# Last two chunks of a gated scan: transposing the input instead of the norm, with a new order of the tail

## The chip, the cores and the metric

The kernel runs on one core of a Trainium2 chip. The metric is the device time of one execution in microseconds; the runs shown have 290.55 us as their median. A core has five engines that each work through their own instructions in order and wait for one another by semaphores: PE (matrix multiplies and transposes, which write to the PSUM banks), DVE (elementwise work and scans), ACT (functions by table, copies), POOL (elementwise work in SBUF) and SP, which here issues the DMA transfers.

## What is computed

Two stages on an input of 4 sequences, 6336 steps and 256 channels. The first is a gated linear recurrence along the steps, the second a gated unit with a causal convolution of 5 taps:

```
log_a = 8 * sigmoid(r_gate) * log(clip(sigmoid(a_param)))
a     = exp(log_a)
norm  = sqrt(max(1 - a*a, 1e-6))
h[t]  = a[t] * h[t-1] + norm[t] * sigmoid(i_gate[t]) * x[t]      # attn_out = all h
gate  = sigmoid(causal_conv(attn_out, conv_w))                   # 5 taps per channel
out   = (gate * (attn_out @ w_val)) @ w_out
```

## The kernel before

The 25344 steps (all sequences in a row) are cut into 51 windows, w0 to w50, of 512 steps (w0, w1 and w50 have 256). The windows form 28 chunks: chunks 0, 1 and 2 have one window each, chunks 3 to 25 have two (w3 and w4, up to w47 and w48), chunk 26 is w49 and chunk 27 is w50. Steps arrive with time on the partitions and channels along the row; the scan needs channels on the partitions, so data is transposed on PE. The 256 channels are two halves h of 128.

Every piece of work is a word in the string ORDER. The kernel goes through the string from left to right and emits each word's instructions; each engine then runs its own words in that order, and waits are inserted where a word reads or overwrites what another engine has not finished. There is no planner at run time: the string is the schedule. A word is a name, its indices and, after @, the PSUM banks (0 to 7) that it fills. For window w, chunk c, half h:

- SP: lr, li, lx load a window of r_gate, i_gate and x (line 290); st.w stores a window of the output (line 519). Each load goes to a ring of 4 windows, each store leaves from a ring of 4.
- ACT: ta.c and tb.c take tanh of half the r and i gates (lines 308 and 311); ex.c.h takes exp out of PSUM into the ring of a (line 376); rt.b takes the square root of 1 - a*a for a batch of chunks (line 403; rt.10 covers chunks 23, 24 and 25, rt.11 chunks 26 and 27); tg.w takes tanh of the convolution (line 475); ca.w copies output out of PSUM (line 508); sa.c.h squares a (line 392). The square root is in another function table than tanh and exp, so each rt is enclosed by two table loads (line 535).
- POOL: pp.w adds one to the i gate (line 318), up.w multiplies it by x into the ring u (line 330), sq.c.h squares a (line 384).
- PE: tr.c.h transposes the r gate (line 355); nt.c transposes the norm back to time on partitions (line 418); xt.c transposes the gated input (line 434); cv.w is the convolution (line 468, 20 matmuls), vl.w the product with w_val (line 483, 4), ou.w the product with w_out (line 498, 8); wm are five matmuls whose result nobody reads (line 362).
- DVE: xg.c multiplies the transposed norm into u (line 425); sc.c.h scans one half of a chunk (line 456, into the ring of y); gv.w combines gate and value (line 488); cd.w copies output out of PSUM (line 506).

Two bfloat16 neighbours are moved as one 32-bit element in the transposes nt and xt, so a window of 512 steps takes 4 of each (two blocks by two halves), one of 256 takes 2.

For each chunk the way from the square root to the scan is: rt (ACT), nt (PE), xg (DVE, PSUM times u into u), xt (PE, into one bank for each half), sc (DVE, which reads a from SBUF and the gated input from PSUM). Then for each window cv and vl on PE, tg on ACT, gv on DVE, ou on PE, a copy, and the store. The y ring holds 3096 columns; chunk 26 starts again at its beginning, where its first scan also copies the last four columns of chunk 25 (line 451).

At the tail, chunks 26 and 27 go through rt.11, nt.26 and nt.27, xg.26 and xg.27, xt.26 and xt.27, sc.26 and sc.27; the last words are w50's: cv.50, tg.50, vl.50, gv.50, ou.50, ca.50, st.50.

Of the kernel before, what the change touches and what calls it, by code (L numbers as in the profile page):

```python
# [42 lines left out]
sc.0.0 up.3 nt.1@3 lx.5 nt.2@0 uv.1 s_wl.0 xg.1 xg.2 xt.1@2,3 lx.7 sc.0.1 lr.12 nt.3@0,1 sc.1.0 lr.11 xt.2@6,7
sc.1.1 ex.5.0 xg.3 tr.5.1@2,3 li.8 sc.2.0 xt.3@0,1 ex.5.1 sq.5.0 cv.0@4,5 sc.2.1 tg.0 sc.3.1 cv.1@6,7 cv.2@2,3 tg.1
tb.4 s_wcast xp.6@6,7 sc.3.0 tg.2 li.10 li.9 pp.5 ta.8 vl.1@4,5 lx.10 vl.2@2,3 uv.6 sq.6.1 vl.0@0,1 ta.7 gv.2 lr.17
cv.3@6,7 lx.8 sq.6.0 gv.0 ou.2.0@2,3 gv.1 tb.5 ou.0.0@0 cd.2.0 ou.1.0@1 up.5 tr.7.0@4,5 tg.3 cd.0.0 st.2 vl.3@2,3
lr.16 cd.1.0 ex.7.0 sq.5.1 st.1 tr.7.1@6,7 gv.3 lr.15 st.0 nt.4@0,1 li.12 ex.7.1 pp.7 cv.4@4,5 xg.4 sq.7.0
# [11 lines left out]
tg.13 sc.9.1 lr.29 pp.20 ou.12.0@0,1 ta.13 up.18 vl.13@6,7 cd.12.0 tr.12.1@3 tg.14 up.17 sc.9.0 st.12 tr.13.1@0,1
ex.12.1 lx.19 lx.20 nt.10@4,5 ex.13.1 li.24 sq.12.1 gv.13 tr.13.0@2,3 tb.12 xg.10 ou.13.0@6,7 sq.13.1 xt.10@4,5  # L60
cd.13.0 ex.13.0 cv.15@0,1 pp.22 sc.10.0 st.13 lx.21 cv.16@6,7 pp.19 lx.22 tg.15 lr.28 lr.30 sq.13.0 vl.15@2,3 tg.16
sc.10.1 li.25 vl.14@0,1 lr.27 pp.21 vl.16@6,7 gv.15 rt.6 sq.14.1 gv.14 ou.15.0@2,3 up.19 gv.16 cv.17@4,5 ou.14.0@0,1
cd.15.0 up.20 ou.16.0@6,7 cd.14.0 st.15 li.26 nt.11@2,3 cd.16.0 sq.14.0 lx.24 vl.17@0,1 tg.17 xg.11 st.14 lx.23
tb.13 st.16 gv.17 xt.11@2,3 up.21 cv.18@4,5 sc.11.1 sc.11.0 li.27 nt.12@0,1 li.28 ta.15 up.22 vl.18@6,7 tg.18 lr.32
pp.23 lr.31 ta.16 ou.17.0@4,5 pp.24 gv.18 up.24 tb.14 xg.12 tr.15.1@2,3 cv.20@6,7 cd.17.0 ex.15.1 xt.12@0,1 up.23
st.17 lr.33 tr.15.0@4,5 sc.12.0 lx.26 tg.20 lr.34 vl.20@2,3 sq.16.1 ex.15.0 cv.19@6,7 sc.12.1 sq.15.1 tg.19
ou.18.0@4,5 tb.15 cd.18.0 cv.21@0,1 pp.26 gv.20 st.18 sq.16.0 vl.19@4,5 tg.21 lx.25 lx.27 nt.13@6,7 ta.17 gv.19
lx.28 li.30 sq.15.0 vl.21@0,1 xg.13 li.29 ou.20.0@4,5 gv.21 xt.13@6,7 pp.27 rt.7 cv.22@2,3 cd.20.0 up.26 ou.21.0@0,1
# [498 lines left out]
```

## Time and profile before

| what | value |
|---|---|
| median of 3 runs | 290.55 us (290.2 to 290.71) |
| the profiled execution | 290.72 us |
| its span, first to last instruction | 288.6 us |
| granted PE clock, mean | 0.996 |
| busy: PE, DVE, ACT, POOL | 250.6, 247.0, 273.7, 241.5 us |
| HBM traffic | 362 GB/s over the span |

The profile is of one execution. Times in it are microseconds from the start of the span; the execution's own time is 2.1 us longer than the span. A row of a timeline gives start, duration, engine, line, operation, output and inputs, and how many instructions are merged; in brackets stands the idle time of the engine before it and what ended that. Instructions of one engine overlap a little, so the time that one holds its engine is read from its start to the next start. A merged row of matmuls is one word or several of the same kind: x8 at line 498 is one ou, x20 at line 468 one cv.

### The profile page before, as it was taken

Reading aid. Unit: us, or ns where it says so; the run is one execution under the profiler, and the core shown is the slowest. Engines: PE = TensorE matmul, PEld = TensorE weight load, DVE = VectorE, ACT = ScalarE, POOL = GpSimd, SP = SyncE. Lnnn points to the kernel's source line nnn. Section 1 sums busy time; section 2 is a strip of 40 time slices with the busy share of each in tenths; the row PEclk is TensorE's granted clock in tenths of the full one; section 3 lists DMA queues with packets and bytes.
Section 4 is the critical chain, followed back from the end, with each engine's and each line's share of the span. In section 5 each row is a group of like instructions: output and inputs, shape, how many; then the busy total and the mean of one; then the engine's idle time right before and its main releaser. Section 6 shows DMA issues by size and latency. Waiting matters only on the chain.

```text
span 288.6 us, 6363 instructions
## 1 busy us (share of the span) xinstructions
PE 250.6 (87%) x2552; PEld 169.4 (59%) x2552; DVE 247.0 (86%) x214; ACT 273.7 (95%) x197; POOL 241.5 (84%) x161
## 2 busy tenths in 40 slices
PE   2397799879898899889898999889799897999993
PEld 1253557547656677466567585467457664676552
DVE  5002899869999999999998999989999999999891
ACT  4999999999999999999999999999999999999754
POOL 1669469999999999999999999999998999496100
PEclk9999999999999999999999999999999999999998
DMA  7999999999999999999999999999999999885554
GB/s 240 396 392 409 407 374 385 357 385 371 403 407 410 410 395 366 375 346 417 418 408 341 376 413 414 418 395 396 351 352 412 420 386 408 263 292 208 199 221 182
DMA packets 29996, 104.76 MB, mean 363 GB/s; under 512 B 3335, under 2 KB 3854, under 8 KB 29966
## 3 DMA queue, kind: packets, MB, share of 16 engines
q1 hardware_dynamic: 29952, 104.35, 93.9%
q8 instruction: 20, 0.33, 0.5%
q14 instruction: 10, 0.08, 0.1%
q10 hardware_dynamic: 14, 0.01, 0.0%
HBM read 78.39 MB, written 25.95 MB: 362 GB/s over the span
## 4 chain that ended last, share of the span: by engine, by line
POOL 31%; PE 20%; DMA 15%; DVE 12%; ACT 12%; issue 7%; SPq 2%; DVEq 0%; ACTq 0%; POOLq 0%
POOL uring L330 14%; POOL ering L384 11%; DMA xring<-in_x_dram 8%; POOL tbring L318 6%; PE banks L468 6%; DMA iring<-in_i_gate_dram 6%; DVE yring L456 5%; DVE tgring L488 4%; PE banks L483 4%; PE banks L498 3%; PE banks L418 3%; ACT aring L376 3%; ACT tbring L311 3%; ACT ering L403 2%; SPq L290 2%
## 5 line engine op out<-in xcount | busy, mean ns | idle before, releaser
L330 POOL TENSOR_TENSOR uring<-tbring,xring 128x1024 bf16<-128x1024 bf16 (+1 forms) x48 | 100.9, 2116 | 11.1 <-DMA xring<-in_x_dram 10.6
L456 DVE TENSOR_TENSOR_SCAN yring<-aring,yring,banks 128x1024 bf16<-128x1024 f32 (+5 forms) x54 | 105.8, 1987 | 0.2
L384 POOL TENSOR_TENSOR ering<-aring 128x1024 f32<-128x1024 f32 (+2 forms) x54 | 91.7, 1715 | 14.7 <-ACT aring L376 14.6
L468 PE MATMUL banks<-yring,diag 64*64 64x512 bf16 (+7 forms) x1080 | 62.9, 361 | 4.6 <-DVE yring L456 3.6
L488 DVE SCALAR_TENSOR_TENSOR tgring<-tgring,banks 128x1024 bf16<-128x1024 bf16 (+1 forms) x51 | 59.3, 1178 | 5.1 <-PE banks L483 2.4
L498 PE MATMUL banks<-wo,tgring 128*128 128x256 bf16 x396 | 51.1, 274 | 7.5 <-DVE tgring L488 4.9
L376 ACT ACTIVATE aring<-banks,khf 128x2048 f32<-128x2048 bf16 (+3 forms) x38 | 53.9, 1467 | 0.4 <-PE banks L355 0.4
L475 ACT ACTIVATE tgring<-banks 128x1024 bf16<-128x1024 f32 (+1 forms) x51 | 50.5, 1007 | 3.0 <-PE banks L468 2.9
L318 POOL TENSOR_SCALAR tbring<-tbring 128x1024 bf16<-128x1024 bf16 (+1 forms) x48 | 49.0, 1030 | 4.4 <-ACT tbring L311 4.3
L498 PEld LDWEIGHTS <-tgring 128*128 128x128 bf16 x396 | 41.4, 114 | 18.6 <-DVE tgring L488 10.5
L483 PE MATMUL banks<-yring,wv 128*128 128x512 bf16 (+4 forms) x216 | 49.6, 361 | 1.6 <-ACT aring L376 0.8
L308 ACT ACTIVATE taring<-rring 128x2048 bf16<-128x2048 f32 (+2 forms) x28 | 47.6, 1718 | 2.4 <-DMA rring<-in_r_gate_dram 2.4
L311 ACT ACTIVATE tbring<-iring 128x2048 bf16<-128x2048 f32 (+2 forms) x28 | 47.9, 1719 | 0.0
L468 PEld LDWEIGHTS <-diag 64*64 64x64 bf16 x1080 | 29.1, 106 | 28.1 <-issue 11.6
L403 ACT ACTIVATE ering<-ering 128x4096 bf16<-128x4096 f32 (+5 forms) x15 | 44.7, 3016 | 0.1
L506 DVE COPY oring<-banks 128x1024 f32<-128x1024 f32 (+1 forms) x36 | 42.0, 1182 | 1.6 <-PE banks L498 1.1
L355 PE MATMUL banks<-ident_b,taring 128*128 128x128 bf16 x396 | 30.2, 230 | 9.4 <-ACT taring L308 7.2
L425 DVE TENSOR_TENSOR uring<-banks,uring 128x2048 bf16<-128x2048 bf16 (+2 forms) x28 | 30.4, 1093 | 6.7 <-PE banks L418 5.7
L355 PEld LDWEIGHTS <-taring 128*128 128x128 bf16 x396 | 26.1, 103 | 15.1 <-ACT taring L308 9.2
L483 PEld LDWEIGHTS <-wv 128*128 128x128 bf16 x216 | 19.9, 98 | 21.3 <-issue 7.1
L418 PE MATMUL banks<-ident,ering 128*128 128x128 f32 x198 | 29.7, 292 | 1.9 <-DVE yring L456 0.9
L418 PEld LDWEIGHTS banks<-ident,ering 128*128 128x128 f32 x198 | 25.9, 207 | 9.1 <-ACT ering L403 3.5
(45 smaller groups left out, 139.7 us busy)
## 6 DMA issues: line engine op xcount, KB each, us to landing
rring<-in_r_gate_dram SPq DMA_DIRECT2D x48, 512.0 KB, 7.9
iring<-in_i_gate_dram SPq DMA_DIRECT2D x48, 512.0 KB, 8.2
xring<-in_x_dram SPq DMA_DIRECT2D x48, 512.0 KB, 7.9
out_dram<-oring SPq DMA_DIRECT2D x48, 512.0 KB, 5.8
rring<-in_r_gate_dram SPq DMA_DIRECT2D x3, 256.0 KB, 4.4
iring<-in_i_gate_dram SPq DMA_DIRECT2D x3, 256.0 KB, 5.8
xring<-in_x_dram SPq DMA_DIRECT2D x3, 256.0 KB, 8.2
out_dram<-oring SPq DMA_DIRECT2D x3, 256.0 KB, 7.4
```

What stands on the lines that cost most here:

```text
L311: nc.scalar.activation(**tangent(c, tbring, NTI, iring, NII))
L318: nc.gpsimd.tensor_scalar(out=t, in0=t, scalar1=1.0, scalar2=1.0, op0=ALU.mult, op1=ALU.add)
L330: nc.gpsimd.tensor_tensor(out=u, in0=t1, in1=xt, op=ALU.mult)
L355: nc.tensor.transpose(out=bank[:, o:o + P], in_=taring[:, place(w, NTR), j, h * P:(h + 1) * P], identity=ident_b[:])
L376: nc.scalar.activation(out=dst, in_=src, func=ACT.Exp, scale=khf[:, h:h + 1], bias=khf[:, h:h + 1])
L384: nc.gpsimd.tensor_tensor(out=e, in0=a, in1=a, op=ALU.mult)
L418: nc.tensor.transpose(out=bank[:, k:k + P], in_=ering[:, e + q:e + wins[w] // 2:nq], identity=ident[:])
L456: nc.vector.tensor_tensor_scan(out=yring[:, h, col:col + o1 - o0], data0=aring[:, h, a_at[c] + o0:a_at[c] + o1], data1=xT[:, o0:o1], initi ...
L468: nc.tensor.matmul(out=gp[oh * 64:oh * 64 + 64, h, a:b], lhsT=diag[half * 64:half * 64 + 64, h, k, :], rhs=yring[half * 64:half * 64 + 64, ...
L483: nc.tensor.matmul(out=val[:, m, a:b], lhsT=wv[:, hk, m * P:(m + 1) * P], rhs=yring[:, hk, col:col + b - a], start=(hk == 0), stop=(hk == ...
L488: nc.vector.scalar_tensor_tensor(out=tgring[:, w % NTG, :, 0:wins[w]], in0=tgring[:, w % NTG, :, 0:wins[w]], scalar=1.0, in1=live.pop(("va ...
L498: nc.tensor.matmul(out=ops[:, j * D:(j + 1) * D], lhsT=gv[:, hk, j:wins[w]:J], rhs=wo[:, hk, :], start=(hk == 0), stop=(hk == H - 1))
```

## The change

For the last two chunks (LAST) the gated input u is transposed first, without the norm: xt.26 and xt.27 put both halves into one PSUM bank. xg.26 and xg.27 then multiply that bank by the norm as it stands (channels on partitions) and write the product into the y ring, at the columns where the chunk's y will stand. The scan reads it from there and overwrites it in place. nt.26 and nt.27 are gone. The other chunks work as before.

The order of the tail is new. Up to w35 each engine has the same words in the same order as before (banks 2, 3 and 4, 5 are exchanged in the middle part, and the words of different engines stand differently in the string). From there on:

- PE: vl.37 directly after nt.22, one new wm.19, and other places for ou, vl and cv up to nt.23; tr.27.0, tr.26.1, tr.27.1 and tr.26.0 later; xt.26 and xt.27 around cv.47, ahead of rt.11's result. From cv.49 on the order is as before.
- POOL: sq.24.0 after sq.25.0; at the end sq.27.0, pp.49, sq.26.1, up.49, pp.50, up.50, sq.26.0 (before: sq.26.1, sq.27.0, sq.26.0, pp.50, pp.49, up.49, up.50).
- ACT: rt.11 after tg.46 and before tg.47 (before: after tb.27 and before ca.42); ta.27, ta.26, the exps of chunks 26 and 27 and tb.27, tb.26 in other places.
- DVE: gv.42, gv.43 and gv.44 spread between the scans of chunks 23 and 24; at the end sc.25.0, sc.25.1, gv.45, gv.46, xg.27, xg.26, sc.26.1, gv.47, sc.26.0, sc.27.0, gv.48, sc.27.1, gv.49, gv.50.
- SP: li.48 ahead of st.36; li.47 and lx.45 behind st.37; lr.50 and lr.49 behind st.38; lx.50 and lx.49 behind st.40, and st.43, st.42, st.44 after them.

The diff, with the order's text from the place where chunk 25 is transposed:

```diff
 NOSB = 4
+LAST = [26, 27]
...
-tr.25.1@0 up.42 ex.25.1 nt.22@4,5 cd.35.0 tg.38 ou.36.0@0,1 sq.24.0 xg.22 sa.25.1 st.35 tr.25.0@6 lr.50 vl.38@2,3
-lx.46 ex.25.0 cd.36.0 pp.43 xt.22@4,5 tb.24 gv.38 st.36 sq.25.0 cv.39@0,1 lx.45 sc.22.0 vl.39@2,3 tg.39 li.47 pp.46
-vl.37@6,7 lr.49 up.43 ou.38.0@0,1 gv.37 rt.10 li.48 cd.38.0 ou.37.0@6,7 pp.45 sc.22.1 vl.40@0,1 up.44 gv.39
-cv.40@4,5 up.46 cd.37.0 nt.23@2,3 st.37 cv.41@6,7 xg.23 tg.40 up.45 lx.48 st.38 lx.47 ta.27 tg.41 nt.24@4,5 gv.40
-vl.41@2,3 xg.24 ta.26 tr.27.0@6 xt.23@0,1 gv.41 ex.27.0 ou.39.0@4,5 tb.25 sc.23.0 cv.42@2,3 ca.39.0 ou.41.0@6,7
-pp.48 tg.42 sc.23.1 st.39 xt.24@4,5 pp.47 li.49 ca.41.0 li.50 tr.26.0@0 ou.40.0@2,3 up.48 ex.26.0 st.41 tr.26.1@6
-sc.24.0 tr.27.1@7 ca.40.0 cv.44@0,1 ex.27.1 up.47 st.40 cv.43@2,3 ex.26.1 lx.49 sc.24.1 tg.44 sa.27.1 nt.25@6,7
-sq.26.1 tg.43 vl.42@0,1 sq.27.0 tb.26 xg.25 vl.44@2,3 sq.26.0 tb.27 vl.43@4,5 gv.42 pp.50 xt.25@6,7 pp.49 gv.44
-ou.42.0@0,1 rt.11 gv.43 ou.44.0@2,3 up.49 ca.42.0 sc.25.1 ou.43.0@4,5 ca.44.0 st.42 cv.45@0,1 ca.43.0 st.44
-cv.46@2,3 sc.25.0 st.43 lx.50 nt.26@7 tg.46 vl.46@4,5 xg.26 tg.45 cv.47@2,3 gv.46 vl.47@0,1 tg.47 ou.46.0@4,5 gv.47
-up.50 vl.45@2,3 ca.46.0 nt.27@0 ou.47.0@6,7 gv.45 st.46 xt.26@4,5 ca.47.0 xg.27 ou.45.0@2,3 sc.26.0 st.47 cv.48@6,7
-ca.45.0 sc.26.1 xt.27@0,1 st.45 tg.48 vl.48@2,3 sc.27.1 cv.49@4,5 gv.48 vl.49@6,7 tg.49 sc.27.0 ou.48.0@2,3 gv.49
-cv.50@4,5 ca.48.0 ou.49.0@6,7 tg.50 st.48 vl.50@2,3 ca.49.0 gv.50 st.49 ou.50.0@2 ca.50.0 st.50
+tr.25.1@0 cd.35.0 nt.22@2,3 up.42 xg.22 ex.25.1 tg.38 vl.37@0,1 sa.25.1 gv.37 tr.25.0@6 st.35 ex.25.0 ou.36.0@4,5
+li.48 cd.36.0 xt.22@2,3 st.36 cv.39@6,7 tb.24 ou.37.0@4,5 wm.19@0 lx.46 vl.38@0,1 sc.22.0 cd.37.0 pp.43 gv.38 tg.39
+sq.25.0 sq.24.0 sc.22.1 cv.40@6,7 st.37 ou.38.0@0,1 rt.10 up.43 vl.39@4,5 vl.40@2,3 cd.38.0 nt.23@0,1 gv.39 pp.46
+up.44 li.47 up.46 pp.45 cv.41@4,5 tg.40 lx.45 xg.23 vl.41@6,7 gv.40 tg.41 gv.41 xt.23@0,1 sc.23.0 st.38 tb.25 up.45
+ou.39.0@2,3 pp.48 lr.50 lx.48 ca.39.0 ou.41.0@6,7 nt.24@4,5 cv.42@2,3 ca.41.0 xg.24 sc.23.1 ou.40.0@6,7 lr.49 lx.47
+st.39 li.50 up.48 pp.47 up.47 tg.42 ta.27 vl.42@4,5 gv.42 ca.40.0 st.41 li.49 xt.24@2,3 tr.27.0@0 cv.43@6,7 ex.27.0
+ta.26 tg.43 vl.43@4,5 sc.24.0 cv.44@0,1 tb.27 tg.44 nt.25@6,7 tr.26.1@2 vl.44@0,1 sq.27.0 st.40 gv.43 ex.26.1 tb.26
+ou.43.0@4,5 xg.25 pp.49 ou.42.0@6,7 tr.27.1@2 ca.43.0 lx.50 lx.49 sq.26.1 up.49 pp.50 gv.44 xt.25@0,1 ca.42.0
+ex.27.1 ou.44.0@4,5 sa.27.1 tr.26.0@2 ca.44.0 sc.24.1 up.50 cv.45@6,7 ex.26.0 sc.25.0 cv.46@4,5 sc.25.1 tg.45 tg.46
+vl.45@2,3 vl.46@6,7 xt.26@4 cv.47@0,1 st.43 sq.26.0 gv.45 gv.46 xt.27@5 st.42 rt.11 tg.47 vl.47@2,3 st.44 xg.27
+xg.26 ou.46.0@6,7 cv.48@4,5 ca.46.0 sc.26.1 st.46 ou.45.0@0,1 vl.48@6,7 gv.47 sc.26.0 ou.47.0@2,3 ca.45.0 tg.48
+sc.27.0 gv.48 sc.27.1 ca.47.0 cv.49@0,1 vl.49@4,5 ou.48.0@6,7 tg.49 ca.48.0 cv.50@0,1 st.45 gv.49 ou.49.0@4,5 st.47
+tg.50 vl.50@6,7 st.48 gv.50 ca.49.0 st.49 ou.50.0@6 ca.50.0 st.50
...
@@ -419,12 +420,37 @@
                         k += P
             live["nT", c] = bank[:, 0:k]
 
+        def y_of(c):
+            ((o0, o1, fresh, col),) = segs[c]
+            return yring[:, :, col:col + clen[c]]
+
+        def op_xt_first(c, at):
+            n = clen[c]
+            for h in range(H):
+                for w in cwins[c]:
+                    nq = wins[w] // (2 * P)
+                    o = (h * n + wstart[w] - cstart[c]) // 2
+                    for q in range(nq):
+                        nc.tensor.transpose(
+                            out=banks[:, at, o + q:o + wins[w] // 2:nq],
+                            in_=uring[:, (w + 1) % NU, q, h * P:(h + 1) * P, :].rearrange("p d two -> p (d two)")
+                            .bitcast(FP32),
+                            identity=ident[:])
+            live["uT", c] = banks[:, at, 0:n].bitcast(BF16).rearrange("p (h n) -> p h n", h=H)
+
         def op_xg(c):
+            if c in LAST:
+                at = 2 * live["n", c]
+                norm = ering[:].bitcast(BF16)[:, at:at + H * clen[c]].rearrange("p (h n) -> p h n", h=H)
+                nc.vector.tensor_tensor(out=y_of(c), in0=live.pop(("uT", c)), in1=norm, op=ALU.mult)
+                return
             u0, nw = (cwins[c][0] + 1) % NU, len(cwins[c])
             u = uring[:, u0:u0 + nw, 0:wins[cwins[c][0]] // (2 * P)].rearrange("p w q d two -> p (w q d two)")
             nc.vector.tensor_tensor(out=u, in0=live.pop(("nT", c)).bitcast(BF16), in1=u, op=ALU.mult)
 
         def op_xt(c, *at):
+            if c in LAST:
+                return op_xt_first(c, at[0])
             for h in range(H):
                 bank = banks[:, at[h]]
                 for w in cwins[c]:
@@ -439,7 +465,7 @@
                 live["xT", c, h] = bank
 
         def op_sc(c, h):
-            xT = live.pop(("xT", c, h)).bitcast(BF16)
+            xT = y_of(c)[:, h] if c in LAST else live.pop(("xT", c, h)).bitcast(BF16)
             for s, (o0, o1, fresh, col) in enumerate(segs[c]):
                 if fresh and h == 0:
                     nc.vector.memset(yring[:, :, col - 4:col], 0.0)
```

More of the change, by code (lines that the diff above doesn't have):

```diff
@@ L43 @@
[L43 to L47, printed above, removed]
@@ new lines @@
+xt.2@6,7 xg.3 ex.5.0 tr.5.1@2,3 li.8 sc.2.0 xt.3@0,1 ex.5.1 cv.0@4,5 sq.5.0 sc.2.1 sc.3.1 cv.1@6,7 tg.0 cv.2@2,3
+tg.1 tb.4 s_wcast xp.6@6,7 sc.3.0 tg.2 li.10 li.9 ta.8 pp.5 lx.10 vl.1@4,5 uv.6 vl.2@2,3 sq.6.1 vl.0@0,1 gv.2 ta.7
+cv.3@6,7 lr.17 lx.8 sq.6.0 gv.0 ou.2.0@2,3 gv.1 tb.5 ou.0.0@0 cd.2.0 ou.1.0@1 up.5 tr.7.0@4,5 cd.0.0 tg.3 st.2
+vl.3@2,3 lr.16 cd.1.0 ex.7.0 tr.7.1@6,7 st.1 sq.5.1 gv.3 lr.15 nt.4@0,1 st.0 li.12 ex.7.1 cv.4@4,5 pp.7 xg.4
+ou.3.0@2,3 sq.7.0 tg.4 vl.4@6,7 cd.3.0 tb.6 xt.4@4,5 pp.8 gv.4 st.3 li.11 sq.7.1 lr.18 sc.4.1 ou.4.0@6,7 li.13 lx.9
@@ L59 @@
[L59 to L68, printed above, removed]
@@ new lines @@
+cd.15.0 ou.16.0@6,7 up.20 cd.14.0 st.15 li.26 nt.11@4,5 cd.16.0 sq.14.0 lx.24 vl.17@0,1 tg.17 xg.11 st.14 lx.23
+tb.13 st.16 gv.17 xt.11@4,5 up.21 cv.18@2,3 sc.11.1 li.27 nt.12@0,1 li.28 ta.15 up.22 vl.18@6,7 sc.11.0 tg.18 lr.32
+pp.23 lr.31 ta.16 ou.17.0@2,3 pp.24 gv.18 up.24 tb.14 xg.12 tr.15.1@4,5 cv.20@6,7 cd.17.0 ex.15.1 xt.12@0,1 up.23
+st.17 lr.33 tr.15.0@2,3 sc.12.0 lx.26 tg.20 lr.34 vl.20@4,5 sq.16.1 ex.15.0 cv.19@6,7 sc.12.1 sq.15.1 tg.19
+ou.18.0@2,3 tb.15 cd.18.0 cv.21@0,1 pp.26 gv.20 st.18 sq.16.0 vl.19@2,3 tg.21 lx.25 lx.27 nt.13@6,7 ta.17 gv.19
@@ new lines @@
+cv.33@0,1 pp.40 ou.32.0@4,5 cd.31.0 up.37 cd.32.0 cv.34@6,7 sc.19.0 nt.20@4,5 up.40 tg.33 lx.41 st.30 tg.34 li.43
+vl.33@0,1 li.44 tb.22 xg.20 vl.34@6,7 pp.39 cv.36@2,3 gv.33 up.39 ta.23 nt.21@4,5 gv.34 ou.33.0@0,1 pp.41 ta.24
+xg.21 lr.48 xt.20@6,7 lr.47 pp.42 st.31 cd.33.0 cv.35@4,5 lx.42 tg.36 sc.20.1 st.32 up.41 tr.23.0@0,1 tg.35
+vl.35@2,3 ex.23.0 li.45 tr.23.1@4,5 gv.35 li.46 ex.23.1 sc.20.0 xt.21@0,1 sq.23.0 st.33 vl.36@2,3 tb.23 ou.34.0@4,5
+sq.24.1 lx.43 gv.36 ou.35.0@6,7 sc.21.0 ca.34.0 cv.37@2,3 pp.44 ta.25 st.34 sq.23.1 cv.38@4,5 lx.44 sc.21.1 tg.37
```

66 lines of the change are left out of this document (33 added, 33 removed).

## The prediction, made before the changed kernel was run

> **What bounds the kernel now.** I started with the chain of waits that ended last: over the last 40 us it runs almost wholly through PE and DVE. So I asked the busy times of that end as two stretches. Columns: stretch, length, then busy us of PE, its weight loads, DVE, ACT, POOL, granted clock, DMA share and GB/s.
>
> ```profile
> 238.40:245.08 6.68, 5.21 (x44) 2.84 (x41) 6.64 (x6) 6.64 (x3) 6.68 (x5) 1.00 1.02 413
> 245.08:278.31 33.23, 33.16 (x337) 22.46 (x336) 31.30 (x25) 30.01 (x32) 17.06 (x13) 1.00 0.70 249
> ```
>
> The bounds are chosen: 245.08 is the start of nt.23, which needs the square root rt.10, and 278.31 that of cv.49. Between them PE is busy 33.16 of 33.23 us. **PE sets that stretch**; DMA has room (0.70) and POOL half. Ahead of it PE idles 1.47 of 6.68 us and ACT sets the pace, ending with rt.10:
>
> ```profile
> 239.70 5.33 ACT L403 ACTIVATE ering<-ering 128x6144 bf16<-128x6144 f32 x1
> ```
>
> It ends at 245.03, and nt.23 starts 0.05 later. The steps of PE, from start to next start, come from its timeline:
>
> ```profile
> 247.45 1.23 PE L418 MATMUL banks<-ident,ering 128*128 128x128 f32 x8
> 248.51 1.03 PE L483 MATMUL banks<-yring,wv 128*128 128x512 bf16 x4
> 249.38 0.28 PE L355 MATMUL banks<-ident_b,taring 128*128 128x128 bf16 x2
> 249.49 1.04 PE L434 MATMUL banks<-ident,uring 128*128 128x128 f32 x8
> 250.37 1.04 PE L498 MATMUL banks<-wo,tgring 128*128 128x256 bf16 x8
> 251.34 1.27 PE L468 MATMUL banks<-yring,diag 64*64 64x512 bf16 x20
> 252.54 1.06 PE L498 MATMUL banks<-wo,tgring 128*128 128x256 bf16 x8
> 253.44 1.04 PE L434 MATMUL banks<-ident,uring 128*128 128x128 f32 x8
> ```
>
> So nt takes 1.06, vl 0.87, two gate transposes 0.11, xt 0.88, cv 1.20; ou 0.97 ahead of a cv and 0.90 ahead of other work.
>
> **The change, part by part.** Removed are nt.26 (four transposes) and nt.27 (two):
>
> ```profile
> 262.66 3.15 PE L498 MATMUL banks<-wo,tgring 128*128 128x256 bf16 x24
> 265.73 2.36 PE L468 MATMUL banks<-yring,diag 64*64 64x512 bf16 x40
> 268.02 0.75 PE L418 MATMUL banks<-ident,ering 128*128 128x128 f32 x4
> 268.61 1.03 PE L483 MATMUL banks<-yring,wv 128*128 128x512 bf16 x4
> ```
>
> ```profile
> 273.38 0.38 PE L418 MATMUL banks<-ident,ering 128*128 128x128 f32 x2
> 273.60 1.04 PE L498 MATMUL banks<-wo,tgring 128*128 128x256 bf16 x8
> ```
>
> Start to start they hold PE 0.59 and 0.22 us: **0.81** together. The input transposes xt.26 and xt.27 stay, four and two instructions, now into one bank each. Every other PE instruction between nt.23 and cv.49 is in both orders, and the set ahead of nt.23 is the same but for wm.19.
>
> The new order also drops a pause. Rows 262.66 and 265.73: three ou take 3.07, where 0.90, 0.90 and 0.97 make 2.77. The chain shows what PE waited for:
>
> ```profile
> 262.33 2.36 DVE tgring L488 x2
> 264.69 0.05 issue
> 264.74 1.07 PE banks L498 x8
> ```
>
> Two gv on DVE, behind xg.25. In the new order gv.42 and gv.43 run long before, and only gv.44 is left there. I take **0.30** for it. From cv.49 on PE's order is the same in both (vl.49, ou.48, cv.50, ou.49, vl.50, ou.50), so what cv.49 gains the end gains: 0.81 + 0.30 = 1.11, cv.49 at 277.2.
>
> That holds only if the other engines hand over in time. I lay the new order out from 245.08 with the steps above. nt.23, cv.41, vl.41, xt.23, ou.39, ou.41, nt.24, cv.42, ou.40, vl.42, xt.24, tr.27.0, cv.43, vl.43, cv.44 make 14.1, so nt.25 runs from 259.2 to 260.4 and tr.26.1 ends at 260.6. From there to the end of cv.46 are nt.25 1.06, tr 0.55, vl 0.87, three ou 2.70, xt.25 0.88, cv 1.10 and 1.27: 267.6. Backward from cv.49, cv.48 starts at 273.3.
>
> DVE from nt.25's end, with its rows:
>
> ```profile
> 260.09 1.20 DVE L425 TENSOR_TENSOR uring<-banks,uring 128x2048 bf16<-128x2048 bf16 x1
> 261.21 3.47 DVE L488 SCALAR_TENSOR_TENSOR tgring<-tgring,banks 128x1024 bf16<-128x1024 bf16 x3
> 264.60 4.58 DVE L456 TENSOR_TENSOR_SCAN yring<-aring,yring,banks 128x1024 bf16<-128x1024 f32 x2
> 269.09 0.67 DVE L425 TENSOR_TENSOR uring<-banks,uring 128x1024 bf16<-128x1024 bf16 x1
> ```
>
> ```profile
> 274.72 0.42 DVE L425 TENSOR_TENSOR uring<-banks,uring 128x512 bf16<-128x512 bf16 x1
> ```
>
> ```profile
> 275.12 3.29 DVE L456 TENSOR_TENSOR_SCAN yring<-aring,yring,banks 128x512 bf16<-128x512 f32 x3
> ```
>
> xg.25 1.12, gv.44 1.13, three scans at 2.25, gv.45 and gv.46 2.26 make 11.3: DVE is free for xg.27 at 271.8. With 0.42 and 0.67 xg.26 ends at 272.8, half a microsecond (0.45) before cv.48 wants its banks. sc.26.1 (about 1.25 of the 3.29), gv.47 and sc.26.0 end at 276.5, 0.7 before cv.49 wants them.
>
> ACT: tg.46 waits for cv.46, 267.7.
>
> ```profile
> 258.55 0.43 ACT L392 ACTIVATE ering<-aring 128x256 f32<-128x256 f32 x1
> 258.86 1.03 ACT L475 ACTIVATE tgring<-banks 128x1024 bf16<-128x1024 f32 x1
> 259.80 1.58 ACT L311 ACTIVATE tbring<-iring 128x1024 bf16<-128x1024 f32 x2
> 261.40 1.28 ACT L535 ACT_TABLE_LOAD   x1
> 262.69 1.49 ACT L403 ACTIVATE ering<-ering 128x1536 bf16<-128x1536 f32 x1
> 264.09 2.82 ACT L508 COPY oring<-banks 128x1024 f32<-128x1024 f32 x3
> ```
>
> With 1.03, 1.28 and 1.49, rt.11 runs from 270.0 to 271.5, 0.3 before DVE is free. The second table load and tg.47 end at 273.8, just before gv.47's turn (274.0). So rt.11 may be 0.3 + 0.45 = **0.75 late for nothing**, then 1:1. Queued behind it are tg.47 (gv.47 waits for that) and the copies of w45 to w47. Before, rt.11 ran at 262.69, with 6 us to spare: this wait is what the change adds.
>
> POOL: sq.26.0, which rt.11 needs, now stands last, behind pp.49, sq.26.1, up.49, pp.50, up.50.
>
> ```profile
> 258.37 2.61 POOL L384 TENSOR_TENSOR ering<-aring 128x512 f32<-128x512 f32 x3
> 261.47 1.63 POOL L318 TENSOR_SCALAR tbring<-tbring 128x512 bf16<-128x512 bf16 x2 [0.48 <-ACT tbring L311]
> 264.22 2.15 POOL L330 TENSOR_TENSOR uring<-tbring,xring 128x1024 bf16<-128x1024 bf16 x1 [1.12 <-DMA xring<-in_x_dram]
> 273.16 1.17 POOL L330 TENSOR_TENSOR uring<-tbring,xring 128x512 bf16<-128x512 bf16 x1 [6.79 <-DMA xring<-in_x_dram]
> ```
>
> tb.26 ends about 262.5 (tr.26.1, an exp under 1 us, tb.26 under 1.1). Two pp 1.63, two up 3.32 and two of the three squares (2.0 of 2.61) make 7.0: sq.26.0 ends at 269.5, **0.5 ahead** of rt.11. up.49 wants its x at 264.5. SP's row of the load of lx.49, and the landing times of all 51 loads of x:
>
> ```profile
> 257.09 0.43 SPq L290 DMA_DIRECT2D xring<-in_x_dram  x1
> ```
>
> ```profile
> DMA to landing us min/median/max: 5.2/7.9/11.4
> ```
>
> Before, lx.49 left at 257.09 and up.49 used it 7.1 us later, as it landed. In the new order it follows st.40 at about 256.8, with lx.50 (256 KB, some 1.05 us at the stretch's 249 GB/s) now ahead of it: 264.9. That is 0.4 late, and 0.5 + 0.75 = 1.25 is free. Likewise li.47 and lx.45 are queued behind st.37 and issue some 4 us later than before; tb.25 and up.45 then start close to their landing, with 1 to 2 us before xg.24 and xg.25 need the products.
>
> At nothing I cost: wm.19, five matmuls 512 wide (some 1.1, as vl's four take 0.87), in PE's 1.47 us of idle time ahead of nt.23, without which vl.38 and the order up to nt.23 move by it; the swapped bank numbers, since the engines' orders up to there are unchanged; and tr.25.0 behind vl.37 (0.2).
>
> Not shown in any row are a multiply into yring in two rows and a scan with both tensors in SBUF, in place. The multiply's neighbours are 0.67 (same size, PSUM and SBUF in) and, at gv's pace, 1.13: +0.8 for both. I take 0.67, the same operation and types. For the scan, two lengths (2.25 for 1024, 1.25 for 512) give some 0.25 of fixed cost; from none of it to twice it is -0.25 to +0.25 each, and I take no change, since the element rate stays that of the recurrence.
>
> The Trainium skill, VectorE: DVE Perf Modes, "The perf-mode tier table (the rule you actually need)", gives any tensor_tensor with a PSUM operand one element per cycle. An estimate from it is about 1.2 us for xg.26, and that is rival two below; the 0.67 us of xg.26 now, with a PSUM input, speaks against it.
>
> **The sum**: 290.72 - 1.11 = 289.6 against the profiled execution (span 288.6). That stands 0.17 above the median of 290.55, so on the median's scale **289.4**.
>
> **The rivals.**
> 1. *The start moves.* PE gains only from 245.08 on. sq.24.0 is now behind sq.25.0, and rt.10 needs both:
>
> ```profile
> 234.44 1.24 ACT L376 ACTIVATE aring<-banks,khf 128x1024 f32<-128x1024 bf16 x1
> 235.98 1.89 POOL L384 TENSOR_TENSOR ering<-aring 128x1024 f32<-128x1024 f32 x1
> ```
>
> ex.25.0 ends at 235.68, two squares of 1.87 end at 239.45; rt.10 starts at 239.70. The 0.25 speaks for the forecast, but whatever is beyond it is lost 1:1, as are small pauses at PE's hand-overs. With 0.75 lost: 290.2, no change.
> 2. *DVE takes PE's place.* Multiplies +0.8 and two scans +0.5 before cv.49, less the 0.7 free: 0.6 lost, 290.0, at the edge of no change.
> 3. *The change shuts POOL behind a load: slower.* If lx.49 lands later than 1.25 us past 264.5, sq.26.0, rt.11, xg.26 and cv.48 follow it 1:1. The gain is gone at 2.4 us late, and it is slower by over 0.58 us from 2.9 us, a landing 10.6 us after issue. At the 11.4 of the longest load seen: 3.7 late, 2.4 lost, 291.8. For it: a median of 7.9, and POOL already waits at both loads. Against: DMA is at 0.70 here, and the long loads are of the full stretches.
> 4. *More goes than I count*: row 264.69 has 0.05 of issue at one hand-over; ten such less in the stretch give 0.5 more, 288.9.
>
> That the change doesn't do what it says is excluded: the norm's transposes of chunks 26 and 27 are no longer issued.
>
> **How the numbers follow.** Forecast 0.60 (own range 288.9 to 289.9), rival 1 0.14, rival 2 0.08, rival 3 0.13, rival 4 0.05. 0.2%, about what a measurement of this kernel can tell from no change, is 0.58 us. Faster: 0.60 + 0.05 + half of rival 2 = 0.69; same: 0.14 + 0.04 = 0.18; slower 0.13. The range runs from 288.6 (rival 4) to 290.9, which takes in rivals 1 and 2 and leaves out rival 3 and a little of 4.
>
> **What would show it.** Right: PE without idle time from nt.23 to cv.49, some 32.1 us; nt.23 still near 245.1; the last six L418 transposes gone; rt.11 starting where the table load ends and DVE going from gv.46 straight into xg.27. Wrong: nt.23 later (rival 1); xg.26 near 1.2 us or the 512-wide scans far from 1.25 (rival 2); POOL idle before up.49 for over 1 us and ACT idle before rt.11 (rival 3). A new idle stretch of PE ahead of cv.48 or cv.49 would make the prediction wrong whichever engine causes it.

## The result

The changed kernel takes 289.01 us (median of 6 runs, 288.62 to 289.94) against 290.58 of the kernel before (6 runs, 290.2 to 291.2). The ratio is 0.9952, with a 95% interval of 0.9931 to 0.9972: about 1.4 us, from 0.8 to 2.0. A second set of runs of the same kernel (below) gave 0.995 (0.9932 to 0.9968). The profiled execution of the changed kernel took 289.94 us with a span of 288.1.

The stretch of the prediction runs from nt.23 to cv.49. In the changed kernel its bounds are 245.53 and 277.77 (columns as in the prediction: stretch, length, busy us of PE, weight loads, DVE, ACT, POOL, clock, DMA share, GB/s):

```profile
245.53:277.77 32.24, 32.02 (x327) 21.90 (x331) 31.02 (x25) 28.92 (x31) 18.78 (x14) 1.00 0.66 248
```

It is 32.24 us here and 32.23 in three more profiles below, against 33.23 before: **1.0 us gone**. PE seems idle for 0.22 us of it; 327 matmuls are recorded, where another run of the same stretch (without wm.19, below) has 332 and no idle time, so I take these for missing records. From cv.49 to the end nothing moved: ou.50, PE's last step, starts 6.08 us after cv.49 in both, at 284.39 before and 283.85 after.

PE's timeline of the changed kernel, with nt.23 and then the tail (a row is start, duration, engine, line, operation; in brackets the idle time ahead of it and what ended it; L419 is nt, L434 the new xt, L494 cv, L509 vl, L524 ou):

```profile
245.53 1.23 PE L419 MATMUL banks<-ident,ering 128*128 128x128 f32 x8 [0.78 <-ACT ering L404]
...
268.25 1.90 PE L509 MATMUL banks<-yring,wv 128*128 128x512 bf16 x7
269.99 0.60 PE L434 MATMUL banks<-ident,uring 128*128 128x128 f32 x4
270.52 1.27 PE L494 MATMUL banks<-yring,diag 64*64 64x512 bf16 x20
271.73 0.44 PE L434 MATMUL banks<-ident,uring 128*128 128x128 f32 x2
272.00 1.03 PE L509 MATMUL banks<-yring,wv 128*128 128x512 bf16 x4
272.86 1.04 PE L524 MATMUL banks<-wo,tgring 128*128 128x256 bf16 x8
273.83 1.27 PE L494 MATMUL banks<-yring,diag 64*64 64x512 bf16 x20
275.04 1.06 PE L524 MATMUL banks<-wo,tgring 128*128 128x256 bf16 x8
275.94 1.03 PE L509 MATMUL banks<-yring,wv 128*128 128x512 bf16 x3
276.80 1.04 PE L524 MATMUL banks<-wo,tgring 128*128 128x256 bf16 x8
277.77 1.27 PE L494 MATMUL banks<-yring,diag 64*64 64x512 bf16 x20
```

The last L419 of the program is now nt.25. Behind nt.23 no row of the stretch waits, and PE goes over from each step to the next.

ACT around rt.11 (L561 is the table load, L404 rt, L501 tg):

```profile
269.41 1.28 ACT L561 ACT_TABLE_LOAD   x1
270.71 1.48 ACT L404 ACTIVATE ering<-ering 128x1536 bf16<-128x1536 f32 x1
```

DVE from gv.45 on (L514 gv, L445 the new xg, L482 scans):

```profile
270.22 2.32 DVE L514 SCALAR_TENSOR_TENSOR tgring<-tgring,banks 128x1024 bf16<-128x1024 bf16 x2
272.47 1.01 DVE L445 TENSOR_TENSOR yring<-banks,ering 128x512 bf16<-128x512 bf16 x2
273.51 1.28 DVE L482 TENSOR_TENSOR_SCAN yring<-aring,yring 128x512 bf16<-128x512 f32 x1
274.71 1.20 DVE L514 SCALAR_TENSOR_TENSOR tgring<-tgring,banks 128x1024 bf16<-128x1024 bf16 x1
275.83 0.15 DVE L477 TENSOR_REDUCE yring<-yring 128x8 bf16<-128x8 bf16 x1
275.90 2.06 DVE L482 TENSOR_TENSOR_SCAN yring<-aring,yring 128x512 bf16<-128x512 f32 x2
```

POOL's last two of interest, up.49 and sq.26.0:

```profile
265.20 2.15 POOL L331 TENSOR_TENSOR uring<-tbring,xring 128x1024 bf16<-128x1024 bf16 x1
...
269.14 1.04 POOL L385 TENSOR_TENSOR ering<-aring 128x512 f32<-128x512 f32 x1
```

rt.11 starts where the table load ends, 0.5 us after sq.26.0 ended; DVE goes from gv.46 into xg.27 without a pause, 0.3 us after rt.11 ended; up.49 waits for no load.

### The profile page after: what moved, and what is told of

Same layout as the page of the kernel before. It is cut to its first block, busy times and chain, and to the rows that moved or that the text cites. A ratio compares the mean times of both kernels' runs of the same rounds, so it can differ in the third digit from the quotient of the medians.

```text
span 288.1 us, 6334 instructions
## 1 busy us (share of the span) xinstructions
PE 247.8 (86%) x2525; PEld 169.0 (59%) x2551; DVE 246.9 (86%) x214; ACT 273.9 (95%) x197; POOL 241.9 (84%) x161
## 4 chain that ended last, share of the span: by engine, by line
POOL 27%; PE 22%; ACT 18%; DVE 13%; DMA 9%; issue 8%; SPq 1%; DVEq 0%; ACTq 0%; POOLq 0%
POOL uring L331 12%; POOL ering L385 9%; DVE yring L482 7%; PE banks L494 6%; POOL tbring L319 5%; PE banks L509 5%; DMA rring<-in_r_gate_dram 5%; PE banks L524 4%; ACT aring L377 4%; ACT ering L404 3%; DMA xring<-in_x_dram 3%; ACT taring L309 3%; ACT tgring L501 3%; DVE tgring L514 3%; ACT tbring L312 2%
## 5 line engine op out<-in xcount | busy, mean ns | idle before, releaser
L482 DVE TENSOR_TENSOR_SCAN yring<-aring,yring,banks 128x1024 bf16<-128x1024 f32 (+5 forms) x50 | 102.1, 2066 | 0.1
L494 PE MATMUL banks<-yring,diag 64*64 64x512 bf16 (+7 forms) x1080 | 62.7, 361 | 3.7 <-DVE yring L482 2.7
L514 DVE SCALAR_TENSOR_TENSOR tgring<-tgring,banks 128x1024 bf16<-128x1024 bf16 (+1 forms) x51 | 59.2, 1178 | 3.4 <-PE banks L509 2.0
L524 PE MATMUL banks<-wo,tgring 128*128 128x256 bf16 x396 | 50.9, 274 | 7.1 <-DVE tgring L514 4.4
L501 ACT ACTIVATE tgring<-banks 128x1024 bf16<-128x1024 f32 (+1 forms) x51 | 50.6, 1009 | 2.5 <-PE banks L494 2.3
L524 PEld LDWEIGHTS <-tgring 128*128 128x128 bf16 x396 | 41.5, 114 | 19.0 <-DVE tgring L514 9.8
L509 PE MATMUL banks<-yring,wv 128*128 128x512 bf16 (+7 forms) x190 | 48.0, 359 | 2.9 <-ACT aring L377 0.8
L404 ACT ACTIVATE ering<-ering 128x4096 bf16<-128x4096 f32 (+5 forms) x15 | 44.7, 3016 | 0.1
L494 PEld LDWEIGHTS <-diag 64*64 64x64 bf16 x1080 | 28.9, 106 | 26.5 <-issue 10.4
L449 DVE TENSOR_TENSOR uring<-banks,uring 128x2048 bf16<-128x2048 bf16 (+2 forms) x26 | 29.4, 1136 | 7.3 <-PE banks L419 6.4
L509 PEld LDWEIGHTS <-wv 128*128 128x128 bf16 x216 | 19.8, 98 | 21.5 <-issue 7.4
L419 PE MATMUL banks<-ident,ering 128*128 128x128 f32 x192 | 28.4, 291 | 2.7 <-ACT ering L404 1.4
L419 PEld LDWEIGHTS banks<-ident,ering 128*128 128x128 f32 x192 | 25.1, 207 | 8.9 <-ACT ering L404 4.2
```

The source lines that it names most:

```text
L482: nc.vector.tensor_tensor_scan(out=yring[:, h, col:col + o1 - o0], data0=aring[:, h, a_at[c] + o0:a_at[c] + o1], data1=xT[:, o0:o1], initi ...
L494: nc.tensor.matmul(out=gp[oh * 64:oh * 64 + 64, h, a:b], lhsT=diag[half * 64:half * 64 + 64, h, k, :], rhs=yring[half * 64:half * 64 + 64, ...
L501: nc.scalar.activation(out=tgring[:, w % NTG, :, 0:wins[w]], in_=live.pop(("gp", w))[:, :, 0:wins[w]], func=ACT.Tanh, scale=0.5)
L509: nc.tensor.matmul(out=val[:, m, a:b], lhsT=wv[:, hk, m * P:(m + 1) * P], rhs=yring[:, hk, col:col + b - a], start=(hk == 0), stop=(hk == ...
L514: nc.vector.scalar_tensor_tensor(out=tgring[:, w % NTG, :, 0:wins[w]], in0=tgring[:, w % NTG, :, 0:wins[w]], scalar=1.0, in1=live.pop(("va ...
L524: nc.tensor.matmul(out=ops[:, j * D:(j + 1) * D], lhsT=gv[:, hk, j:wins[w]:J], rhs=wo[:, hk, :], start=(hk == 0), stop=(hk == H - 1))
```

## The experiments

The theory: PE's work sets the stretch from nt.23 to cv.49, rt.10 on ACT sets its start, and the gain is PE work that is gone. The rival readings: the gain lies elsewhere (the new front of the order, the start, the copies of work ahead), or it is the order that gains and the transposes count for nothing. Line numbers shift by one where the order's text is a line shorter.

**The changed kernel once more**, to see how far its time and its stretch repeat.

> The changed kernel unchanged, with more runs. Theory: PE sets the stretch from nt.23 to cv.49, and the change takes 0.81 us of transposes and a 0.30 us pause out of it, nothing else; the stretch is 32.2 to 32.3 us again and the time 1.0 to 1.2 us below before. What the medians show beyond that (1.57) is then a difference in the run-up to nt.23 that comes and goes from run to run: nt.23 starts anywhere from 244.2 to 245.6. Rival: the change also gains about 0.5 us in the run-up itself; then the time is 1.5 us or more below before over many runs, and nt.23 starts below 244.8 in most profiles of the new order.

Measured: 289.36 us (288.42 to 289.84), ratio 0.995 (0.9932 to 0.9968). The profiled run began the stretch 1.06 us earlier (nt.23 at 244.47), and the stretch was 32.23 again. The start varies from run to run; the stretch doesn't.

**The new way alone, in the order of before.**

```diff
-st.43 lx.50 nt.26@7 tg.46
+st.43 lx.50 xt.26@7 tg.46
...
-ca.46.0 nt.27@0 ou.47.0@6,7 gv.45 st.46 xt.26@4,5 ca.47.0 xg.27 ou.45.0@2,3
+ca.46.0 ou.47.0@6,7 gv.45 st.46 ca.47.0 ou.45.0@2,3
...
-xt.27@0,1 st.45 tg.48 vl.48@2,3 sc.27.1
+xt.27@0 st.45 tg.48 vl.48@2,3 xg.27 sc.27.1
```

> The new way for chunks 26 and 27 in the order of before (xt.26 in the place of nt.26, xt.27 in its old place, nt.27 gone). Theory: the transposes go, the pause behind gv.44 and gv.43 stays: the stretch from nt.23 to cv.49 is 0.8 us shorter than before (32.4), the time 0.7 to 0.9 us below before. Rival, the new order is what gains: no change against before, within 0.3 us.

Measured: 290.3 us, ratio 0.999 (0.9976 to 1.0005); the stretch is 33.12, only 0.11 shorter. The expectation failed, and the rows of this kernel say why. PE of the kernel before, then of this one (L498 and L523 are ou; the last row of each is ou.45):

```profile
274.47 0.60 PE L434 MATMUL banks<-ident,uring 128*128 128x128 f32 x4
274.91 1.04 PE L498 MATMUL banks<-wo,tgring 128*128 128x256 bf16 x8
```

```profile
272.56 1.03 PE L508 MATMUL banks<-yring,wv 128*128 128x512 bf16 x4
273.42 1.04 PE L523 MATMUL banks<-wo,tgring 128*128 128x256 bf16 x8
274.90 1.07 PE L523 MATMUL banks<-wo,tgring 128*128 128x256 bf16 x8 [0.44 <-DVE tgring L513]
```

DVE of this kernel, gv.47 and gv.45:

```profile
271.98 1.22 DVE L513 SCALAR_TENSOR_TENSOR tgring<-tgring,banks 128x1024 bf16<-128x1024 bf16 x1 [0.97 <-ACT tgring L500]
273.62 1.22 DVE L513 SCALAR_TENSOR_TENSOR tgring<-tgring,banks 128x1024 bf16<-128x1024 bf16 x1 [0.41 <-PE banks L508]
```

In the order of before vl.45 (272.56) stands late, gv.45 waits for it (0.41), and ou.45 waits for gv.45. Before, nt.27 and xt.26 filled that time on PE; taken away, they leave 0.44 us of waiting, and ou.45 starts 29.69 us after nt.23 (245.21 here) where it started 29.83 after before. PE was busy 33.16 of 33.23 us before, but part of that work only covered a chain PE - DVE - PE. "Busy" was not "bound".

**The new order alone**, with the norm transposed as before (LAST empty; nt.26 and nt.27 directly after vl.47, the old xt.26 and xt.27 behind xg). On PE cv.48 and vl.48 move too: behind nt.27 stand ou.46, xt.26, ou.45, cv.48, xt.27, ou.47, vl.48. On DVE xg.26 stands ahead of xg.27.

```diff
-LAST = [26, 27]
+LAST = []
-vl.47@2,3 st.44 xg.27 xg.26 ou.46.0@6,7 cv.48@4,5
+vl.47@2,3 nt.26@4 nt.27@5 st.44 xg.26 xg.27 ou.46.0@6,7 xt.26@4,5
```

> The new order with the old way for chunks 26 and 27: nt.26 and nt.27 behind vl.47, then xg, xt.26, scans, xt.27; the banks of the last words are changed to have room. Theory: the order needs the short way. rt.11 ends near 272.2, and nt.26, xg.26 and xt.26 now stand between it and sc.26.1, which starts some 2.5 us later than in the changed kernel; cv.49 follows with it: 2 to 3 us above the changed kernel, 0.8 to 1.5 us above before. Rival, the order alone gains: at or below before.

Measured: 291.41 us, ratio 1.0025 (1.0013 to 1.0036): slower than before. The stretch is 33.84. Its DVE:

```profile
272.82 1.02 DVE L448 TENSOR_TENSOR uring<-banks,uring 128x1024 bf16<-128x1024 bf16 x2 [0.63 <-PE banks L418]
274.37 1.28 DVE L481 TENSOR_TENSOR_SCAN yring<-aring,yring,banks 128x512 bf16<-128x512 f32 x1 [0.53 <-PE banks L459]
```

With rt.11 this late, the old way has two turns on PE (nt, then xt) between the square root and the scan, and DVE waits for both. From cv.49 to ou.50 it takes 0.45 us more as well. So neither half, as tried here, pays alone: in the stretch the way gives -0.11, the order +0.61, both together -1.0. I read it so: the new way lets rt.11 be late, and with rt.11 late the order has room to bring vl.45 and gv.45 ahead of rt.11, so that no wait appears where the transposes were. That last link was not tried by itself, and with cv.48 and vl.48 moved too the +0.61 is not the order's alone.

**More PE work in the changed kernel**: five matmuls whose result nobody reads, between cv.46 and vl.45.

```diff
-cv.46@4,5
+cv.46@4,5 wm.20@3
```

> The changed kernel with one more wm (five matmuls that nobody reads, some 1.08 us) between cv.46 and vl.45. Theory: PE sets the stretch, so its length grows by 1.0 to 1.1 us and the time with it, 0.5 us or less below before. Rival, DVE or ACT already set the stretch of the changed kernel: growth under 0.5 us.

Measured: 290.22 us, ratio 0.9993 (0.9982 to 1.0004).

```profile
244.42:277.73 33.31, 33.09 (x331) 22.38 (x335) 31.39 (x25) 29.02 (x31) 18.79 (x14) 1.00 0.64 242
```

The stretch grew by 1.08 us; the five matmuls take 1.09 from start to next start. In the new order PE work at this place counts one to one.

**Without wm.19.**

```diff
-wm.19@0
```

> The changed kernel without wm.19. Theory: it stands in PE's idle time ahead of nt.23, so the stretch stays 32.2 us and the time within 0.2 us of the changed kernel's. Rival: it keeps something going, or its 1.1 us is on the path; then nt.23 starts over 0.3 us earlier against rt.10, or the clock or the stretch changes.

Measured: 289.39 us, ratio 0.9955 (0.9938 to 0.9972): no change. PE waits instead for a gv (1.14) and for rt.10 (0.83) ahead of nt.23. This profile has all its records in the stretch, 332, and in them PE has no idle time at all:

```profile
244.22:276.45 32.23, 32.23 (x332) 21.90 (x332) 30.96 (x25) 28.91 (x31) 18.77 (x14) 1.00 0.67 250
```

**The front of the new order alone**: the order as after up to tr.25.1, from there the order and the way of before.

```diff
-LAST = [26, 27]
+LAST = []
-tr.25.1@0 cd.35.0 nt.22@2,3 up.42
+tr.25.1@0 up.42 ex.25.1 nt.22@4,5
...
```

> The changed kernel's order up to w35 (banks exchanged, words of different engines in another sequence, each engine's own words as before), then the old tail and the old way. Theory: the run-up to nt.23 differs only by chance from run to run, so the time is that of before, within 0.15 us in the median, and the stretch is 33.1 to 33.3 us. Rival: the front gains by itself; then the median is 0.25 us or more below before, with ACT never waiting for a load of r between the start of tb.4 and rt.10 (200.17 us between them, against 200.45 before).

Measured: 290.24 us, ratio 0.9995 (0.998 to 1.001); the stretch is 33.22. The front by itself gains nothing that can be told.

**A later start**: ACT's square of chunk 25, head 1, is written twice over.

```diff
-sa.25.1
+sa.25.1 sa.25.1
```

> The changed kernel with ScalarE's square of chunk 25, head 1 (0.95 us of ScalarE's time after its overlap), written twice over, so that ScalarE reaches the square root of chunks 23 to 25 (rt.10) later; the same values are computed. Theory (rt.10 on ScalarE sets the start of the stretch, and all behind it slides with it): nt.23 comes 0.8 to 1.0 us later against the load that ends ScalarE's run-up, PE's stretch from nt.23 to cv.49 stays 32.2 (at most 0.3 shorter, where VectorE's and GpSimd's gained time takes up waits of PE), and the time lies 0.6 to 1.0 above the changed kernel: 290.0 to 290.3. Rival (the start is not what counts; another engine, VectorE above all, which runs without a pause from 228 to 246, sets the pace of the tail): the stretch shortens by about as much as the start is late, and the time is that of the changed kernel within 0.3.

Measured: 290.25 us, ratio 0.9992 (0.9972 to 1.0012). ACT of this kernel, the two squares and rt.10:

```profile
234.03 2.18 ACT L392 ACTIVATE ering<-aring 128x1024 f32<-128x1024 f32 x2
...
241.33 5.33 ACT L403 ACTIVATE ering<-ering 128x6144 bf16<-128x6144 f32 x1
```

Counted from the start of tb.4, where ACT's run-up begins, rt.10 comes 201.26 us later, against 200.17 in the changed kernel: 1.09, as long as the second square with what follows it, and 0.1 more than the highest figure expected. The stretch is untouched:

```profile
246.71:278.94 32.23, 32.01 (x327) 21.90 (x331) 30.82 (x25) 28.91 (x31) 18.77 (x14) 1.00 0.64 239
```

DVE, which works without a pause from 228 to 246 in the changed kernel, did not hold the tail back: rt.10 sets the start, and what is lost there is lost at the end.

**Chunk 25 the new way too**, with its product over two banks and its transposes in other places.

```diff
-LAST = [26, 27]
+LAST = [25, 26, 27]
-ex.27.0 ta.26 tg.43 vl.43@4,5 sc.24.0 cv.44@0,1 tb.27 tg.44 nt.25@6,7 tr.26.1@2
+ex.27.0 xt.25@0,1 ta.26 tg.43 vl.43@4,5 sc.24.0 cv.44@6,7 tb.27 tg.44 tr.26.1@2
...
-pp.50 gv.44 xt.25@0,1 ca.42.0
+pp.50 gv.44 ca.42.0
```

> The changed kernel with chunk 25 done the new way too: nt.25 gone, xt.25 ahead of vl.43, the banks of cv.44, vl.44 and ou.43 changed. Theory: in the new order PE sets the stretch, so taking 1.06 us of transposes from it shortens it until DVE takes over, which has 0.6 us of room and loses its 0.6 us wait in front of xg.25: 0.6 to 0.9 us below the changed kernel, a stretch of 31.3 to 31.6. Rival: sc.25.0 and sc.25.1, which now read both inputs from SBUF while POOL works on up.49, up.50 and sq.26.0, and these POOL instructions hold one another up; then scans or POOL instructions of that time are longer or later by 1 us or more, and the time is at the changed kernel's or above. The Trainium skill, SBUF, Who interferes with whom, has this as its rule: of a DVE instruction with two SBUF inputs and a GpSimd instruction that reads SBUF, the second to start waits for the whole of the first.

Measured: 293.55 us, ratio 1.0088 (1.0061 to 1.0115): 4 us slower than the changed kernel, although nt.25's eight transposes (1.06 us of PE) are gone. The rival came in, not the theory. DVE (the two scans of chunk 25), POOL (up.49 and pp.50) and ACT (rt.11):

```profile
264.33 2.33 DVE L482 TENSOR_TENSOR_SCAN yring<-aring,yring 128x1024 bf16<-128x1024 f32 x1
...
266.57 4.17 DVE L482 TENSOR_TENSOR_SCAN yring<-aring,yring 128x1024 bf16<-128x1024 f32 x1
```

```profile
264.42 4.18 POOL L330 TENSOR_TENSOR uring<-tbring,xring 128x1024 bf16<-128x1024 bf16 x1
268.57 2.59 POOL L318 TENSOR_SCALAR tbring<-tbring 128x512 bf16<-128x512 bf16 x1
```

```profile
273.43 1.49 ACT L403 ACTIVATE ering<-ering 128x1536 bf16<-128x1536 f32 x1 [3.66 <-POOL ering L384]
```

A scan that takes both inputs from SBUF and POOL's work beside it take turns. The first scan started ahead of up.49 and took its usual 2.33. up.49 started 0.09 later and took 4.18 where 2.15 is usual; the second scan started inside up.49 and took 4.17; pp.50 started inside that scan and took 2.59 and not 0.62. Each time the one that starts second takes its usual time and all but 0.2 us of what was left of the other, so it waits for the first, as the rival has it. The scan just ahead, at 262.08 with its input in PSUM, ran beside two POOL instructions, and all three took their usual times (2.34, 1.04, 1.04). sq.26.0 is POOL's last, so rt.11 waits 3.66 us.

**Five chunks the new way.**

```diff
-LAST = [26, 27]
+LAST = [23, 24, 25, 26, 27]
-nt.23@0,1 gv.39 pp.46 up.44 li.47
+gv.39 pp.46 up.44 xt.23@0,1 li.47
...
-ou.41.0@6,7 nt.24@4,5 cv.42@2,3
+ou.41.0@6,7 xt.24@4,5 cv.42@2,3
```

> The changed kernel with chunks 23, 24 and 25 done the new way as well (nt.23 and nt.24 replaced by xt.23 and xt.24 in their places, the later xt gone). Theory: PE loses another 2.1 us, which DVE lets through only in part (0.2 to 0.5 us, its idle time ahead of xg.23 and xg.24): a stretch of 30.9 to 31.5, 0.8 to 1.3 us below the changed kernel. Rival as for the kernel with chunk 25, and larger, since eight more instructions of POOL, up and pp, run beside the scans of chunks 23 and 24: 1 to 6 us above the changed kernel, with scans or up instructions longer than 2.33 and 2.16 us.

Measured: 299.72 us, ratio 1.0302 (1.0267 to 1.0338). Groups of DVE from 245 to 285 and of POOL in the same time (count, then busy us and mean ns of one, then idle time):

```profile
L482 DVE TENSOR_TENSOR_SCAN yring<-aring,yring 128x1024 bf16<-128x1024 f32 x6 | 19.1, 3214 | 0.0
```

```profile
L330 POOL TENSOR_TENSOR uring<-tbring,xring 128x1024 bf16<-128x1024 bf16 x5 | 12.7, 2543 | 0.2
L318 POOL TENSOR_SCALAR tbring<-tbring 128x1024 bf16<-128x1024 bf16 x4 | 9.8, 2447 | 6.2 <-ACT tbring L311 6.1
```

Three chunks are spared their nt, and 10 us are lost, more than the rival's 1 to 6: the six scans take 2.34 to 4.18 us, 3.2 on average, POOL is slowed beside them, and rt.11, at 281.54, waits 5.39 us for POOL's last square.

**The same trouble, made in the changed kernel**: three products of POOL are repeated behind its last square, beside the scans of chunks 26 and 27.

```diff
-sq.26.0
+sq.26.0 up.47 up.48 up.47
```

> The changed kernel with three products of GpSimd repeated at the end of its work, behind the last square (the gated inputs of windows 47, 48 and 47 again, into places whose readers are done; the same values are computed): each is 2.15 us alone, so GpSimd works from 270.2 to about 276.7, beside the scans of chunks 26 and 27, which read both inputs from SBUF. Theory (a scan that reads two inputs from SBUF and GpSimd hold each other up): the 512-wide scans take 2 to 2.6 us and not 1.28, the repeated products 3 to 4.2 and not 2.15, cv.49 comes 0.3 to 1.5 later and the time is 0.3 to 1.5 above the changed kernel. Rival (the long scans of the wider uses had their own cause, such as the 1024-wide form or the banks): scans at 1.28, products at 2.15, and a time within 0.3 of the changed kernel.

Measured: 290.16 us, ratio 0.9979 (0.9958 to 1.0); about 0.8 us above the changed kernel by the two ratios, whose intervals touch; the stretch is 33.02, 0.79 longer. DVE's groups, POOL's with the third product by itself, and PE at cv.49:

```profile
L481 DVE TENSOR_TENSOR_SCAN yring<-aring,yring 128x512 bf16<-128x512 f32 x2 | 3.9, 1940 | 0.0
L481 DVE TENSOR_TENSOR_SCAN yring<-aring,yring 128x256 bf16<-128x256 f32 x2 | 1.5, 749 | 0.0
```

```profile
L330 POOL TENSOR_TENSOR uring<-tbring,xring 128x1024 bf16<-128x1024 bf16 x3 | 7.3, 2462 | 0.0
...
273.44 3.08 POOL L330 TENSOR_TENSOR uring<-tbring,xring 128x1024 bf16<-128x1024 bf16 x1
```

```profile
277.65 1.27 PE L493 MATMUL banks<-yring,diag 64*64 64x512 bf16 x20 [0.72 <-DVE yring L481]
```

The two 512-wide scans take 1.94 us on average (1.95 and 1.93) and not 1.28. Of POOL's products only the third, which starts inside a scan, takes longer (3.08); the two that start ahead of the scans take their usual 2.15, so 2.46 on average stays below the 3 to 4.2 expected. PE now waits for the scan ahead of cv.49. The rival failed: the long scans come from POOL's work beside them and not from the wider form, since the trouble appears in the changed kernel itself as soon as POOL still works at that time.

## Why the prediction came out

The forecast was 289.4, a gain of 1.11; measured are 289.01 and, in the second set, 289.36.

- **PE sets the stretch.** Right for the changed kernel (1.08 us more PE work, 1.08 more stretch; no idle time where all records are there). For the kernel before it was argued too simply: "PE is busy 33.16 of 33.23" was taken as a bound, and the new way alone shows that some of that work hid a wait. The forecast didn't fall over it because the change moves vl.45 and gv.45 as well.
- **0.81 for nt.26 and nt.27, 0.30 for the pause.** Together 1.11; the stretch lost 1.0. By kind of step in the two timelines, from start to next start, all nt of the stretch take 3.28 us and not 4.09: 0.81, as laid out. The ou take 8.10 and not 8.52 and the vl 7.04 and not 7.11, together 0.49 less, where the pause was put at 0.30. But the cv take 9.54 and not 9.40, the gate transposes 0.85 and not 0.76, the xt 3.43 and not 3.35, together 0.31 more: for one, two cv that stood in a row (2.29) now stand apart and take 1.21 and 1.20. That leaves about 0.2 for the second term. It came close because its two errors, a gain put too small and hand-overs of the new order put at nothing, partly cancel; that is luck in a small way.
- **The hand-overs to the other engines.** All as laid out, within 0.1: sq.26.0 0.5 ahead of rt.11 (0.5), rt.11 0.3 ahead of DVE (0.3), xg.26 0.35 ahead of cv.48 (0.45), sc.26.0 0.6 ahead of cv.49 (0.7).
- **wm.19, banks, tr.25.0 at nothing.** Right for wm.19, by the run without it, and within 0.15% for the banks of the middle part, by the front alone; tr.25.0 was not tried by itself.
- **xg and scan unchanged.** The new xg takes 677 ns (1024 wide) and 414 (512), against 674 and 422 before; the scan in place 1278 ns against 1263 from PSUM. But the reason given for the scan ("the element rate stays that of the recurrence") was only half of it. It holds while POOL is idle. POOL's last instruction ended at 270.18 and the first such scan began at 273.51, since rt.11 waits for that instruction. The prediction didn't have this among its rivals; laid beside POOL's work the same scans cost 0.79 us. That POOL was done came with the order and not from the prediction's reasoning, so here it was lucky.
- **Rival 1, the start.** sq.24.0 ended at 239.96, 0.2 before rt.10 started at 240.16 (laid out: 0.25), so rt.10 wasn't held up by it. That a later start costs one to one is shown by the doubled square.
- **Rival 2, DVE.** The Trainium skill, VectorE: DVE Perf Modes, "The perf-mode tier table (the rule you actually need)", would have put xg.26 at about 1.2 us (estimate in the prediction); the 677 ns disagree, also with the output in yring.
- **Rival 3, POOL behind a load.** up.49 started without a wait. **Rival 4, more goes**: no, in the stretch.

What the stretch doesn't explain: the ratio speaks of 1.4 us, 0.4 more, though its interval begins at 0.8. Two things on record fit. From tb.4 to rt.10 eight profiles in the new order take 200.12 to 200.18 us (without the one with the doubled square), the two in the order of before 200.45 and 200.56. In each of those two ACT waits once for a load of r, at different places (0.22 us at 44.08 before, 0.32 at 167.92 in the new way alone), and in none of the other ten profiles. ACT before:

```profile
44.08 1.92 ACT L308 ACTIVATE taring<-rring 128x2048 bf16<-128x2048 f32 x1 [0.22 <-DMA rring<-in_r_gate_dram]
```

And the execution's time is longer than the span by 1.80 to 1.88 us in the new order (medians of each set of runs), by 1.93 and 1.94 in the way alone and the front alone, and by 1.98 to 2.05 in the three sets of the kernel before. The front alone has no wait for a load of r either and 200.27 on the first count, yet no gain that could be measured (0.9995, 0.998 to 1.001); that interval has room for 0.2 us. Whether the order removes that wait or the loads landed early by chance, and what makes the time outside the span, **stays open**.

## What to carry to other kernels

An engine that is busy all the time isn't yet a bound: before you subtract work from it, look for a chain that leaves the engine and comes back, and ask whether the removed work was what covered it. A shorter path from a late result to its user is worth most together with an order that uses it by making that result late; here neither was worth anything alone. When a scan's input moves from PSUM to SBUF, look at what POOL does at that time before you extend the trick to more of the kernel.

## What the runs showed of the hardware

That a scan with both inputs in SBUF and POOL hold each other up was not in the prediction. The one that started first took its usual time, and the other took its own and all but 0.2 us of the rest of the first: a 512-wide scan went from 1.28 to 1.94 us, a 1024-wide one from 2.33 to as much as 4.18; POOL's product from 2.15 to 4.18, its addition of 512 from 0.62 to 2.59. Scans with one input in PSUM take 2.33 in the main loop, where POOL works nearly all the time. The Trainium skill, SBUF — State Buffer, "Who interferes with whom", says that a VectorE instruction with two SBUF inputs contends with a GpSimd instruction that reads SBUF, and one with at most one, outside the 2-port perf modes, does not. These runs agree.
